# First block's attention for all 512 tokens ahead of the feed-forward, with the second q piece loaded before v

## The chip, the cores and the metric

The kernel runs on one core of a Trainium2 chip. The metric is device time in microseconds (us), the median of several runs of the same kernel. A profiled execution gives the trace from which all rows below are taken.

## The reference

Two stages: attention with keys and values projected along the sequence (1024 positions to 64), then a two-layer feed-forward net with a sigmoid-weighted gelu. There are 8 batches, 8 heads, 1024 positions, head size 64; the feed-forward goes from 512 to 2048 and back.

```python
k_proj = np.einsum('ks,bhsd->bhkd', E, k)
v_proj = np.einsum('ks,bhsd->bhkd', F, v)
scores = scale * np.matmul(q, k_proj.transpose(0, 1, 3, 2))
attn = np.exp(scores - max); attn = attn / (sum(attn) + 1e-09)
x = np.matmul(attn, v_proj)          # heads side by side: 8192 tokens x 512
h = x @ w_in                         # 512 -> 2048
out = (h * (1.0 / (1.0 + np.exp(-1.702 * h)))) @ w_out   # 2048 -> 512
```

## The kernel before

The 8192 tokens are worked in 16 blocks of 512 (index `j` or `h`), two blocks to a batch. A block's attention gives `xT`, 512 features by 512 tokens, in four chunks, one for each pair of heads (`p`). `ffn1` (L377) makes one of 16 feature chunks (`fc`) of the hidden layer with four matmuls over `w_in` and a gelu on ACT. `ffn2` (L395) sums over the 16 chunks with `w_out` for one of four token groups (`n`), and ACT copies the result out.

The schedule is written by hand. The code emits instructions in program order, and each engine works through its own queue in that order. `fill` and `at(j, slot, ...)` (L424 to L507) put attention work of later blocks between the feed-forward steps of block `j`: a slot is the index of an `ffn1` step, or `O`/`Q` plus the index of an `ffn2` part. Tiles in PSUM come from two pools of four buffers each, `ps_f` (`f_tile`) and `ps_x`; a tile that takes a used buffer waits until its reader is done.

Loads are issued by POOL through one queue, in the order of L91 to L106: k in three pieces, the first quarter of q's positions (two of eight), v in three pieces, the second quarter of q, six of eight pieces of `w_in`, the rest of q, the last two pieces of `w_in`, four pieces of `w_out`, then the loads of batch 1. A load is issued when the one eight places earlier has landed.

Block 0 has a start of its own (L431 to L471). `k_piece` projects and transposes k, `q_tr0(g, u, cp)` (L235) transposes a quarter of q on PE, `scores(0, u, half)` (L275) makes scores and exps for 256 tokens, and `v_piece` (L206) projects v for some heads and writes it, masked, into `vx` tiles that have a column of ones behind each head's 64 values. `tok(h, p, half)` (L349) multiplies the exps with `vx` for one pair of heads and two groups of 128 tokens. That gives values and sums together; DVE takes the reciprocal (L359) and multiplies (L361). `x_tr` (L364) transposes the result into `xT` (L369, L371). `warm(n)` (L141) issues matmuls over zeros.

Before the feed-forward starts, only the first 256 tokens (half 0) go through this. Block 0's `ffn1` then runs on half blocks (256 columns): twelve chunks of half 0, twelve of half 1, and so on (L458). The attention of half 1 is placed between the first ones (L459 to L462). The first two chunks of half 0 use a tanh form of the gelu (L390 to L393), while the exp table is still loaded on ACT. The gelu table is loaded after the exps of half 1 (`gelu_table`, L292).

Block 0's `ffn2` begins with two token groups in turn over chunks 0 to 7, 8 to 11 and 12 to 15 (L521).

Batch 1's k is transposed by a DMA on SP's queue (`kv_out`, L229), behind the transposes of its q (`q_dma`, L259). The first reader is `scores(2, ...)`, at the end of block 1's `ffn1`.

Of the kernel before, what the change touches and what calls it, by code (L numbers as in the profile page):

```python
# [9 lines left out]
F32 = mybir.dt.float32  # L10
BF16 = mybir.dt.bfloat16
AF = mybir.ActivationFunctionType
ALU = mybir.AluOpType
# [4 lines left out]
def kernel(ctx, tc, q, k, v, E, F,  # L18
                                                     moe_w_in, moe_w_out, out):
    nc = tc.nc  # L20
    B, H, S, D = q.shape
    KP, _ = E.shape
    DM, DFF = moe_w_in.shape
    P = 128
    J = S // P
    NB2 = S // 512
    HP = H // 2
    KC = DM // P
    FC = DFF // P
    TB = 512  # L30
    JB = TB // P
    NBLK = B * S // TB
    scale = 1.0 / float(D) ** 0.5
# [16 lines left out]
    kt, vt, qt = {}, {}, {}  # L50

    def load_kv(src, dst, b, name, hs=H, js=0, jn=J):
        if b not in dst:
            dst[b] = ldpool.tile([P, H, J, D], BF16, name=name)
        sv = src[b].rearrange("h (p j) d -> p h j d", p=P)
        for h, n in [(h, hs) for h in range(0, H, hs)] if isinstance(hs, int) else hs:
            nc.gpsimd.dma_start(out=dst[b][:, h:h + n, js:js + jn], in_=sv[:, h:h + n, js:js + jn])  # L57
# [35 lines left out]
    make_identity(nc, ident)  # L93
    qt[0] = q_buf(0)
    load_kv(q, qt, 0, "", H, 0, 2)
    load_kv(v, vt, 0, "v_sb", ((0, 4), (4, 2), (6, 2)))
    load_kv(q, qt, 0, "", H, 2, 2)
    for i in range(6):
        load_w_in(i)
    load_kv(q, qt, 0, "", H, JB, JB)  # L100
# [37 lines left out]
    def f_tile(shape, dt=F32):  # L138
        return ps_f.tile(shape, dt, name="f_ps")

    def warm(n):  # L141
        w_ps = ps_x.tile([P, TB], F32, name="x_ps")
        for _ in range(n):
            nc.tensor.matmul(w_ps, zeros[:, :P], zeros, start=True, stop=True)  # L144

# [55 lines left out]
    def vx_of(b, p):  # L201
        if b == 1:
            return vx1[:, 2 * p:2 * p + 2]
        return vx0[0][:, 2 * p:2 * p + 2] if p < 2 else vx0[p - 1]

    def v_piece(h0, n):  # L206

        v_ps = proj0(1, h0, n)
        if n == 4:
            nc.vector.tensor_tensor(vx0[0][:, :, :D], v_ps, mask, op=ALU.mult)  # L210
        else:
            for t in range(n):
                nc.scalar.activation(vx_of(0, h0 // 2)[:, t, :D], v_ps[:, t, :], AF.Identity,
                                     scale=rows[:, h0 % 4 + t:h0 % 4 + t + 1])
# [60 lines left out]
    def scores(h, u, half=None, x=False):  # L275
        b, c = divmod(h, NB2)
        j0, n = (c * JB, JB) if half is None else (c * JB + half * JB // 2, JB // 2)
        ts = slice(j0 * P - c * TB, (j0 + n) * P - c * TB)

        def go():  # L280
            if h not in expT:
                expT[h] = att.tile([P, HP, TB], BF16, name="expT", bufs=3)
            s_ps = [(x_tile() if x else f_tile([P, TB]))[:, :n * P] for _ in range(2)]
            eight(s_ps, [kts[b % 2][:, 2 * u + i, :] for i in range(2)],
                 [q0s[half][u][:, :, i, :] if h == 0 else qT[b][:, j0:j0 + n, 2 * u + i, :]
                   for i in range(2)])
# [59 lines left out]

    xs = {}

    def tok(h, p, half):  # L349
        def go():  # L350
            d_ps = f_tile([P, 4, D + 1]) if (h, half) == (0, 0) and p > 1 else                 ps_x.tile([P, 4, D + 1], F32, name="x_ps")
# [9 lines left out]
            nc.vector.tensor_tensor(xs[h, p, half], d_ps[:, :, :D], rd.to_broadcast([P, 4, D]), op=ALU.mult)  # L361
        return go

    def x_tr(h, p, half):  # L364
        def go():
            x_sb = xs.pop((h, p, half)).rearrange("s (i t) d -> s i (t d)", i=2)
            n_ps = ps_x.tile([P, 2, P], BF16, name="x_ps")
            for i in range(2):
                nc.tensor.transpose(n_ps[:, i, :], x_sb[:, i, :], ident)  # L369
            cp = nc.scalar.copy if (h, half) == (0, 0) else nc.vector.tensor_copy  # L370
            cp(x_of(h)[:, p, half * TB // 2:(half + 1) * TB // 2], n_ps.rearrange("r i s -> r (i s)"))  # L371
        return go


# [2 lines left out]
    def ffn1(j, fc, ts=slice(0, TB)):  # L377
        if j not in gts:
            gts[j] = work.tile([P, FC, TB], BF16, name="gT")
        n = ts.stop - ts.start  # L380
        h_ps = f_tile([P, n])
        for kc in range(KC):
            nc.tensor.matmul(h_ps, w_in_sb[:, kc, fc * P:(fc + 1) * P], xT[j][:, kc, ts],  # L383
                             start=(kc == 0), stop=(kc == KC - 1))
        if j > 0 or ts.start > 0 or fc > 1:
            nc.scalar.activation(gts[j][:, fc, ts], h_ps, AF.Gelu_apprx_sigmoid)  # L386
        else:

            t_sb = work.tile([P, n], F32, name="t_sb", bufs=3)
            nc.scalar.activation(t_sb, h_ps, AF.Tanh, scale=0.851)  # L390
            g = gts[j][:, fc, ts]
            nc.vector.scalar_tensor_tensor(g, t_sb, 1.0, h_ps, op0=ALU.add, op1=ALU.mult)
            nc.vector.tensor_scalar_mul(g, g, 0.5)  # L393

    def ffn2(j, n, fcs):  # L395
        b, c = divmod(j, NB2)
# [29 lines left out]
    def at(j, slot, *fs):  # L426
        fill.setdefault((j, slot), []).extend(fs)

    O = FC
    Q = 2 * FC  # L430
    for h0, n in ((0, 4), (4, 2), (6, 2)):  # L431
        k_piece(h0, n)
    DV, AC = nc.vector.tensor_copy, nc.scalar.copy
# [1 line left out]
    q_tr0(0, 1, AC)  # L435
    warm(2)
    for u in range(2):
        scores(0, u, 0)()
    warm(4)
    v_piece(0, 4)  # L440
    warm(3)
    for p in range(2):
        tok(0, p, 0)()
    v_piece(4, 2)
    warm(1)
    x_tr(0, 0, 0)()
    warm(1)
    tok(0, 2, 0)()
    x_tr(0, 1, 0)()
    v_piece(6, 2)  # L450
    warm(1)
    x_tr(0, 2, 0)()
    tok(0, 3, 0)()
    x_tr(0, 3, 0)()
    q_tr0(1, 0, DV)
    q_tr0(1, 1, DV)

    order = [(half, fc) for fcs in (range(12), range(12, FC)) for half in range(2) for fc in fcs]  # L458
    at(0, 1, scores(0, 0, 1), scores(0, 1, 1, True), gelu_table)  # L459
    for p in range(HP):  # L460
        at(0, 2 + p, tok(0, p, 1))
        at(0, 5 + p, x_tr(0, p, 1))  # L462
    at(0, 20, q_tr(2))
    at(0, 23, q_tr(3))
    for u in range(2):
        at(0, Q, scores(1, u, None, u > 0))
    at(0, Q + 1, gelu_table)
    for p in range(HP):
        at(0, Q + (2, 4, 6, 7)[p], tok(1, p, 0), tok(1, p, 1))
        at(0, Q + (4, 6, 7, 8)[p], x_tr(1, p, 0), x_tr(1, p, 1))  # L470
    at(1, 9, proj(1), kv_out(1))  # L471
    at(1, 1, q_dma(1, 0, JB), q_dma(1, JB, JB))
    for u in range(2):
# [82 lines left out]
```

The softmax here doesn't subtract the row's maximum and nothing guards it: scores larger than these inputs give would overflow.

## Time and profile before

| What | us |
|---|---|
| Median of 7 runs (510.4 to 511.76) | 510.93 |
| The profiled execution's own time | 511.09 |
| Its span, first to last instruction | 509.3 |
| PE busy | 502.6 |
| L415 (`ffn2` matmuls), PE busy, 1008 of them | 226.7 |
| L383 (`ffn1` matmuls), PE busy, 1088 of them | 225.7 |
| ACT busy | 263.7 |
| DVE busy | 158.3 |
| Mean granted TensorE clock | 1.00 |

In the rows that follow, a timeline line has the start in us, the duration in us, the engine, the source line, the operation, the tile written and the tiles read, the shape and a count. A bracket at its end tells how long the engine was idle before it and what ended that. A chain line has start, duration and what ran. "PEld" is PE's weight load, which runs beside matmuls. A matmul's duration in the timeline includes its way through the array; the distance between starts is what a stream of them costs.

### The profile page before, as it was taken

The numbers are of one execution on the slowest core, as the hardware profiler recorded it, in microseconds if no ns is written. First come the engines' busy times: TensorE is split into PE (matmuls) and PEld (weight loads), VectorE is DVE, ScalarE is ACT, GpSimd is POOL, SyncE is SP. The second block draws the span as 40 slices with busy tenths as digits, with TensorE's granted clock in tenths as the row PEclk, the third lists the DMA queues.
The fourth block names the chain that finished last, engine by engine and source line by source line (L and its number), as shares of the span: only waits on it lengthen the run. The fifth ranks groups of instructions, "written<-read, shape, count | busy, mean of one in ns | idle before, by whom it ended". The sixth has DMA issues, their size and how long they took to land.

```text
span 509.3 us, 7242 instructions
## 1 busy us (share of the span) xinstructions
PE 502.6 (99%) x3094; PEld 232.2 (46%) x3094; DVE 158.3 (31%) x219; ACT 263.7 (52%) x443; POOL 78.0 (15%) x97
## 2 busy tenths in 40 slices
PE   8999999999999999999999999999999999999997
PEld 4585445444444444444444444444444444444444
DVE  4523114607161623216161331616214161611000
ACT  1675562664637365471746637374563737244351
POOL 7442051510600510041000510000000000000000
PEclk9999999999999999999999999999999999999999
DMA  9999999999999997598938969090603205060202
GB/s 166 197 203 207 213 157 186 223 200 130 141 239 256 113 195 143 136 154 91 228 62 211 115 111 230 9 244 1 171 1 73 95 5 162 1 167 1 82 1 82
DMA packets 125737, 68.77 MB, mean 135 GB/s; under 512 B 92629, under 2 KB 116565, under 8 KB 123785
## 3 DMA queue, kind: packets, MB, share of 16 engines
q0 software_dynamic: 84400, 29.37, 50.8%
q1 hardware_dynamic: 41224, 38.69, 30.2%
q8 instruction: 24, 0.39, 0.3%
q10 hardware_dynamic: 80, 0.26, 0.2%
q14 instruction: 9, 0.07, 0.0%
HBM read 72.88 MB, written 16.99 MB: 176 GB/s over the span
## 4 chain that ended last, share of the span: by engine, by line
PE 92%; DMA 6%; POOL 1%; issue 0%; DVE 0%; ACT 0%; POOLq 0%
PE f_ps L415 43%; PE f_ps L383 42%; PE f_ps L174 3%; DMA w_in_sb<-in_moe_w_in_dram 2%; DMA v_sb<-in_v_dram 2%; PE f_ps L269 2%; PE x_ps L269 1%; DMA kt<-k_b 1%; PE f_ps L407 1%; PE x_ps L307 1%; POOL k_sb L57 0%; PE x_ps L354 0%; PE x_ps L369 0%; PE f_ps L251 0%; POOL q_even L57 0%
## 5 line engine op out<-in xcount | busy, mean ns | idle before, releaser
L415 PE MATMUL f_ps<-w_out_sb,gT 128*128 128x512 bf16 x1008 | 226.7, 379 | 0.0
L383 PE MATMUL f_ps<-xT,w_in_sb 128*128 128x512 bf16 (+1 forms) x1088 | 225.7, 367 | 0.6 <-ACT gT L386 0.3
L386 ACT ACTIVATE gT<-f_ps 128x512 bf16<-128x512 f32 (+1 forms) x270 | 151.7, 574 | 58.8 <-PE f_ps L383 57.5
L383 PEld LDWEIGHTS <-w_in_sb 128*128 128x128 bf16 x1088 | 105.7, 98 | 116.1 <-DMA w_in_sb<-in_moe_w_in_dram 0.9
L415 PEld LDWEIGHTS <-gT 128*128 128x128 bf16 x1008 | 95.7, 98 | 121.7 <-issue 11.8
L418 ACT COPY o_sb<-f_ps 128x512 f32<-128x512 f32 x63 | 36.9, 586 | 130.7 <-PE f_ps L415 121.0
L342 DVE TENSOR_TENSOR xT<-x_ps,rbc 128x512 bf16<-128x512 f32 x52 | 33.3, 685 | 217.6 <-PE x_ps L269 120.7
L310 DVE RECIPROCAL rden<-x_ps 128x512 f32<-128x512 f32 x26 | 85.3, 3322 | 10.4 <-PE x_ps L307 10.3
L70 POOL DMA_DIRECT2D q_sb<-in_q_dram x48 | 42.0, 905 | 154.9 <-DMA qT<-q_sb 131.3
L288 ACT ACTIVATE expT<-f_ps 128x512 bf16<-128x512 f32 (+1 forms) x58 | 30.1, 573 | 30.4 <-PE f_ps L269 30.3
L288 ACT ACT_TABLE_LOAD x13 | 16.7, 1283 | 4.7 <-PE f_ps L269 4.5
L292 ACT ACT_TABLE_LOAD x14 | 18.0, 1283 | 0.3
L57 POOL DMA_DIRECT2D k_sb<-in_k_dram x10 | 8.5, 857 | 54.8 <-PE f_ps L174 53.1
L228 DVE CAST k_b<-f_ps 64x512 bf16<-64x512 f32 x7 | 4.8, 683 | 37.8 <-PE f_ps L174 37.8
L174 PE MATMUL f_ps<-k_sb,eft 128*64 128x512 bf16 x56 | 13.4, 382 | 0.0
L174 PE MATMUL f_ps<-v_sb,eft 128*64 128x512 bf16 x56 | 13.4, 382 | 0.0
L144 PE MATMUL x_ps<-zeros 128*128 128x512 bf16 x34 | 11.4, 459 | 1.2 <-DVE zeros L115 1.2
L409 DVE COPY o_sb<-f_ps 128x256 f32<-128x256 f32 (+1 forms) x2 | 0.7, 358 | 37.3 <-issue 36.9
L269 PE MATMUL f_ps<-qT,kt 64*32 64x512 bf16 x208 | 10.6, 386 | 0.4 <-DMA kt<-k_b 0.4
L269 PE MATMUL x_ps<-expT,vq 64*32 64x512 bf16 x208 | 10.2, 378 | 0.0
L361 DVE TENSOR_TENSOR x_sb<-x_ps,rd 128x256 bf16<-128x256 f32 x22 | 9.3, 425 | 0.8
L359 DVE RECIPROCAL rd<-x_ps 128x4 f32<-128x4 f32 x22 | 3.8, 175 | 17.8 <-PE x_ps L354 17.8
(71 smaller groups left out, 128.3 us busy)
## 6 DMA issues: line engine op xcount, KB each, us to landing
out_dram<-o_sb SPq DMA_DIRECT2D x15, 1024.0 KB
rbc<-rdr SPq DMA_DIRECT2D x26, 512.0 KB
k_sb<-in_k_dram POOLq DMA_DIRECT2D x7, 1024.0 KB, 14.0
v_sb<-in_v_dram POOLq DMA_DIRECT2D x7, 1024.0 KB, 18.2
q_sb<-in_q_dram POOLq DMA_DIRECT2D x48, 128.0 KB, 5.5
w_in_sb<-in_moe_w_in_dram POOLq DMA_DIRECT2D x8, 256.0 KB, 12.2
w_out_sb<-in_moe_w_out_dram POOLq DMA_DIRECT2D x4, 512.0 KB, 14.7
q_even<-in_q_dram POOLq DMA_DIRECT2D x8, 128.0 KB, 10.2
```

The costliest lines, as they stand in the source:

```text
L70: nc.gpsimd.dma_start(out=qt[b][:, j], in_=qv[:, j])
L144: nc.tensor.matmul(w_ps, zeros[:, :P], zeros, start=True, stop=True)
L174: nc.tensor.matmul(kvps[b][r], eft(j, slice(e * KP, (e + 1) * KP)), (kt, vt)[e][b][:, :, j, :], start=(j == 0), stop=(j == J - 1))
L269: nc.tensor.matmul(outs[i][r.start + c:r.start + c + 32], lhsTs[i][ri, c:c + 32], rhss[i][ri], start=True, stop=True)
L288: nc.scalar.activation(expT[h][:, 2 * u + i, ts], s_ps[i], AF.Exp, scale=scale)
L292: nc.scalar.preload_act_table(AF.Gelu_apprx_sigmoid)
L310: nc.vector.reciprocal(rden[:, e, :], d_ps[e])
L342: nc.vector.tensor_tensor(x_of(h)[:, 2 * u + i, :], n_ps[i], rbc[h][:, 2 * u + i, :], op=ALU.mult)
L383: nc.tensor.matmul(h_ps, w_in_sb[:, kc, fc * P:(fc + 1) * P], xT[j][:, kc, ts], start=(kc == 0), stop=(kc == KC - 1))
L386: nc.scalar.activation(gts[j][:, fc, ts], h_ps, AF.Gelu_apprx_sigmoid)
L415: nc.tensor.matmul(o_ps[n], gts[j][:, fc, n * P:(n + 1) * P], w_out_sb[:, fc, :], start=(fc == 0), stop=(fc == FC - 1))
L418: nc.scalar.copy(osb[j][:, n, :], o_ps.pop(n))
```

## The change

- The second quarter of q is loaded ahead of v.
- Scores and exps of half 1 move ahead of v's projection, and so does the load of the gelu table.
- The sums of the exps are computed by matmuls of their own with the ones columns (two columns wide), for two token groups and all pairs at a time (`sums0`); DVE takes 16 reciprocals per partition at once.
- The values come from `tok0`, one pair of heads and all four token groups at a time, with two multiplications on DVE. `x_tr0` transposes four groups, copied by ACT in one piece for pairs 0 to 2, by DVE in two pieces for pair 3.
- Block 0's `ffn1` has two half-width chunks for each half, then 14 whole ones. The tanh form is gone.
- Block 0's `ffn2` begins with three token groups in turn, by quarters of the chunks. The slots of block 1's attention and of the later q transposes are moved to fit.

```diff
     load_kv(q, qt, 0, "", H, 0, 2)
+    load_kv(q, qt, 0, "", H, 2, 2)
     load_kv(v, vt, 0, "v_sb", ((0, 4), (4, 2), (6, 2)))
-    load_kv(q, qt, 0, "", H, 2, 2)
...
-    def warm(n):
-        w_ps = ps_x.tile([P, TB], F32, name="x_ps")
+    def warm(n, f=False):
+        w_ps = f_tile([P, TB]) if f else ps_x.tile([P, TB], F32, name="x_ps")
...
+    rd0 = consts.tile([P, 2, HP, 2, 2], F32, name="rd0")
+
+    def sums0(half):
+        d_ps = ps_x.tile([P, HP, 2, 2], F32, name="x_ps")
+        for p in range(HP):
+            for i in range(2):
+                t = 2 * half + i
+                nc.tensor.matmul(d_ps[:, p, i, :], expT[0][:, p, t * P:(t + 1) * P],
+                                 vx_of(0, p)[:, :, D:].rearrange("r t o -> r (t o)"), start=True, stop=True)
+        nc.vector.reciprocal(rd0[:, half], d_ps)
+
+    def tok0(p):
+        n_ps = ps_x.tile([P, 2, 2, 2, D], F32, name="x_ps")
+        for t in range(JB):
+            nc.tensor.matmul(n_ps[:, t // 2, t % 2].rearrange("s t d -> s (t d)"),
+                             expT[0][:, p, t * P:(t + 1) * P], vx_of(0, p)[:, :, :D], start=True, stop=True)
+        xs[p] = work.tile([P, 2, 2, 2, D], BF16, name="x0_sb", bufs=4)
+        for a in range(2):
+            nc.vector.tensor_tensor(xs[p][:, a], n_ps[:, a], rd0[:, a, p, :, :, None].to_broadcast([P, 2, 2, D]),
+                                    op=ALU.mult)
+
+    def x_tr0(p, parts, cp):
+        n_ps = ps_x.tile([P, JB, P], BF16, name="x_ps")
+        for g in range(parts):
+            for t in range(g * JB // parts, (g + 1) * JB // parts):
+                nc.tensor.transpose(n_ps[:, t, :], xs[p][:, t // 2, t % 2].rearrange("s t d -> s (t d)"), ident)
+            sl = slice(g * JB // parts, (g + 1) * JB // parts)
+            cp(x_of(0)[:, p, sl.start * P:sl.stop * P], n_ps[:, sl].rearrange("r t s -> r (t s)"))
...
-        if j > 0 or ts.start > 0 or fc > 1:
-            nc.scalar.activation(gts[j][:, fc, ts], h_ps, AF.Gelu_apprx_sigmoid)
-        else:
...
+        nc.scalar.activation(gts[j][:, fc, ts], h_ps, AF.Gelu_apprx_sigmoid)
...
-    Q = 2 * FC
+    order = [(half, fc) for half in range(2) for fc in range(2)] + [(None, fc) for fc in range(2, FC)]
+    Q = len(order)
...
     for u in range(2):
-        scores(0, u, 0)()
-    warm(4)
-    v_piece(0, 4)
-    warm(3)
-    for p in range(2):
-        tok(0, p, 0)()
-    v_piece(4, 2)
-    warm(1)
-    x_tr(0, 0, 0)()
-    warm(1)
-    tok(0, 2, 0)()
-    x_tr(0, 1, 0)()
-    v_piece(6, 2)
-    warm(1)
-    x_tr(0, 2, 0)()
-    tok(0, 3, 0)()
-    x_tr(0, 3, 0)()
+        scores(0, u, 0, u > 0)()
     q_tr0(1, 0, DV)
     q_tr0(1, 1, DV)
-    order = [(half, fc) for fcs in (range(12), range(12, FC)) for half in range(2) for fc in fcs]
-    at(0, 1, scores(0, 0, 1), scores(0, 1, 1, True), gelu_table)
+    warm(1)
+    sums0(0)
+    for u in range(2):
+        scores(0, u, 1, u > 0)()
+    gelu_table()
+    v_piece(0, 4)
+    sums0(1)
+    warm(1, True)
+    tok0(0)
+    tok0(1)
+    v_piece(4, 2)
+    warm(2, True)
+    x_tr0(0, 1, AC)
+    tok0(2)
+    v_piece(6, 2)
+    warm(1, True)
+    x_tr0(1, 1, AC)
+    tok0(3)
+    warm(1, True)
+    x_tr0(2, 1, AC)
+    warm(1, True)
+    x_tr0(3, 2, DV)
+    warm(2, True)
+    at(0, 13, q_tr(2))
+    at(0, 15, q_tr(3))
+    for u in range(2):
+        at(0, Q + 1, scores(1, u, None, True))
+    at(0, Q + 3, gelu_table)
     for p in range(HP):
-        at(0, 2 + p, tok(0, p, 1))
-        at(0, 5 + p, x_tr(0, p, 1))
-    at(0, 20, q_tr(2))
-    at(0, 23, q_tr(3))
...
-        at(0, Q + (2, 4, 6, 7)[p], tok(1, p, 0), tok(1, p, 1))
-        at(0, Q + (4, 6, 7, 8)[p], x_tr(1, p, 0), x_tr(1, p, 1))
+        at(0, Q + (4, 6, 9, 11)[p], tok(1, p, 0), tok(1, p, 1))
+        at(0, Q + (6, 9, 11, 12)[p], x_tr(1, p, 0), x_tr(1, p, 1))
...
-            parts[:4] = [(n, fcs) for fcs in (range(8), range(8, 12), range(12, FC)) for n in range(2)]
+            parts[:6] = [(n, range(4 * g, 4 * g + 4)) for g in range(4) for n in range(3)]
```

More of the change, by code (lines that the diff above doesn't have):

```diff
@@ L347 @@
     xs = {}
+    rd0 = consts.tile([P, 2, HP, 2, 2], F32, name="rd0")
[23 more added lines that the diff above has]
+            cp(x_of(0)[:, p, sl.start * P:sl.stop * P], n_ps[:, sl].rearrange("r t s -> r (t s)"))
     def tok(h, p, half):
         def go():
-            d_ps = f_tile([P, 4, D + 1]) if (h, half) == (0, 0) and p > 1 else                 ps_x.tile([P, 4, D + 1], F32, name="x_ps")
+            d_ps = ps_x.tile([P, 4, D + 1], F32, name="x_ps")
             for i in range(2):
@@ L369, in go @@
                 nc.tensor.transpose(n_ps[:, i, :], x_sb[:, i, :], ident)
-            cp = nc.scalar.copy if (h, half) == (0, 0) else nc.vector.tensor_copy
-            cp(x_of(h)[:, p, half * TB // 2:(half + 1) * TB // 2], n_ps.rearrange("r i s -> r (i s)"))
+            nc.vector.tensor_copy(x_of(h)[:, p, half * TB // 2:(half + 1) * TB // 2], n_ps.rearrange("r i s -> r (i s)"))
         return go
@@ L384, in ffn1 @@
                              start=(kc == 0), stop=(kc == KC - 1))
-        if j > 0 or ts.start > 0 or fc > 1:
-            nc.scalar.activation(gts[j][:, fc, ts], h_ps, AF.Gelu_apprx_sigmoid)
-        else:
[L389 to L393, printed above, removed]
+        nc.scalar.activation(gts[j][:, fc, ts], h_ps, AF.Gelu_apprx_sigmoid)
     def ffn2(j, n, fcs):
@@ L437 @@
     for u in range(2):
-        scores(0, u, 0)()
-    warm(4)
-    v_piece(0, 4)
-    warm(3)
-    for p in range(2):
-        tok(0, p, 0)()
-    v_piece(4, 2)
-    warm(1)
-    x_tr(0, 0, 0)()
-    warm(1)
-    tok(0, 2, 0)()
-    x_tr(0, 1, 0)()
-    v_piece(6, 2)
-    warm(1)
-    x_tr(0, 2, 0)()
-    tok(0, 3, 0)()
-    x_tr(0, 3, 0)()
+        scores(0, u, 0, u > 0)()
     q_tr0(1, 0, DV)
     q_tr0(1, 1, DV)
-    order = [(half, fc) for fcs in (range(12), range(12, FC)) for half in range(2) for fc in fcs]
-    at(0, 1, scores(0, 0, 1), scores(0, 1, 1, True), gelu_table)
-    for p in range(HP):
-        at(0, 2 + p, tok(0, p, 1))
-        at(0, 5 + p, x_tr(0, p, 1))
-    at(0, 20, q_tr(2))
-    at(0, 23, q_tr(3))
[L465 to L468, printed above, removed]
-        at(0, Q + (2, 4, 6, 7)[p], tok(1, p, 0), tok(1, p, 1))
-        at(0, Q + (4, 6, 7, 8)[p], x_tr(1, p, 0), x_tr(1, p, 1))
+    warm(1)
[26 more added lines that the diff above has]
+    at(0, Q + 3, gelu_table)
+    for p in range(HP):
+        at(0, Q + (4, 6, 9, 11)[p], tok(1, p, 0), tok(1, p, 1))
+        at(0, Q + (6, 9, 11, 12)[p], x_tr(1, p, 0), x_tr(1, p, 1))
     at(1, 9, proj(1), kv_out(1))
```

## The prediction

> **What bounds the kernel now.** I read the page's busy shares first, then the chain of waits in order of time, then the timeline of the first 30 us on PE and POOL, and last the busy time by stage.
>
> ```profile
> span 509.3 us, 7242 instructions
> PE 502.6 (99%) x3094; PEld 232.2 (46%) x3094; DVE 158.3 (31%) x219; ACT 263.7 (52%) x443; POOL 78.0 (15%) x97
> PE 92%; DMA 6%; POOL 1%; issue 0%; DVE 0%; ACT 0%; POOLq 0%
> ```
>
> PE is the bound nearly everywhere, so a change at the start is worth what it moves the moment from which PE runs without a gap, plus the PE work that it takes out after that moment. The chain in order of time shows where PE is not the bound:
>
> ```profile
> 5.73 10.46 DMA v_sb<-in_v_dram
> 16.47 11.50 DMA w_in_sb<-in_moe_w_in_dram
> 28.02 4.98 PE f_ps L383 x44
> ...
> 55.42 8.63 PE f_ps L383 x40
> ...
> 66.68 6.60 DMA kt<-k_b
> ```
>
> Up to 28.02 us transfers decide: first v, then w_in. From 28.02 on it is PE, with one later transfer on the chain, kt at 66.68 us. On PE, the last steps before the first feed-forward matmul (L383) are these:
>
> ```profile
> 14.89 1.05 PE L182 MATMUL f_ps<-v_sb,ffs 128*128 128x256 bf16 x8
> ...
> 20.36 0.29 PE L369 MATMUL x_ps<-ident,x_sb 128*128 128x128 bf16 x2 [0.74 <-DVE x_sb L361]
> ...
> 21.28 1.05 PE L383 MATMUL f_ps<-xT,w_in_sb 128*128 128x256 bf16 x8
> ```
>
> The first v projection starts at 14.89, ended by the wait for v; the feed-forward starts at 21.28. POOL issues a load only when an earlier one has landed, so its releasers tell when each landed:
>
> ```profile
> 12.61 0.74 POOL L86 DMA_DIRECT2D w_in_sb<-in_moe_w_in_dram  x1 [0.69 <-DMA q_even<-in_q_dram]
> 15.12 0.74 POOL L86 DMA_DIRECT2D w_in_sb<-in_moe_w_in_dram  x1 [1.78 <-DMA v_sb<-in_v_dram]
> 16.47 0.74 POOL L86 DMA_DIRECT2D w_in_sb<-in_moe_w_in_dram  x1 [0.60 <-DMA v_sb<-in_v_dram]
> 17.77 0.89 POOL L57 DMA_DIRECT2D q_even<-in_q_dram  x1 [0.56 <-DMA v_sb<-in_v_dram]
> 20.19 0.75 POOL L86 DMA_DIRECT2D w_in_sb<-in_moe_w_in_dram  x1 [1.54 <-DMA q_even<-in_q_dram]
> ```
>
> The reader is to see the steps: v's three pieces let go at 15.12, 16.47 and 17.77, the second q piece only at 20.19. The busy time by stage (elapsed us, then busy us of PE, PEld, DVE, ACT, POOL):
>
> ```profile
> 21.28:38.98 17.70, 17.12 (x193) 14.35 (x193) 6.33 (x20) 13.69 (x36) 8.43 (x11) 1.00 1.37 201
> 38.98:55.25 16.27, 16.27 (x114) 8.13 (x112) 6.16 (x24) 6.91 (x11) 4.03 (x5) 1.00 1.48 196
> ```
>
> Block 0's first feed-forward layer takes 17.70 us, its second 16.27, the latter without a gap.
>
> **What the Trainium skill says.** "ScalarE: Activation LUTs", section "Table sets", says that cheap functions such as identity and copy are in every table set, and "What ACT_TABLE_LOAD costs" gives 1283 ns and a drain of about 1380 ns. The trace has 1283 ns at L292 (23.87) and the next gelu at 25.17, so no drain shows; I take 1.28 us, and no reload for the copies that follow the moved load. "DMA: Bandwidth & Descriptors", section "Queues, rings and completion order", says that each engine takes turns among its rings. This bears on the instruction queue: the trace shows one q8 packet of 0.02 MB between 17.3 and 17.5 us, and the q piece then in flight took 2.42 us from step to step (17.77 to 20.19), where the first q piece of the same size took 1.43 (11.18 to 12.61). I charge about 1 us of that to this packet. "TensorE: Matmul & The Clock Gate", section "The HAM clock gate", says that about 3.4 us of idle halve PE's clock. The trace's PE waits 0.74 us before 20.36 and the granted clock stays 1.00.
>
> **The change part by part.** *Saved after the start.* Of the 17.70 us, the half-width matmuls are 128, at 0.111 each (44 in 28.02 to 32.92). The two q transposes cost 2 x 0.57. The rest, 2.3 us, is block 0's second token half (scores, four toks, four transposes, about 1.5 us) and waits (about 0.8: the gelu table, w_in). After: 16 half-width matmuls (1.78), 56 whole ones at 0.2157 (8.63/40, so 12.08), the same q transposes (1.14): 15.0 us. Saved: 2.70 us. A w_in piece is now used in 1.73 us against one arriving every 1.35, so no w_in wait follows if the start is after 21.3. w_out's first quarter releases POOL at 36.66; it is needed 15.0 us after the start, at 38 or later. The tanh form of gelu for two tiles goes, six small instructions with two gelus in their place; ACT and DVE hid them beside PE, so it counts nothing. The second layer in three token groups by quarters has the same 64 matmuls: 16.27 stays. Its scores use four x_ps buffers; ACT frees them (1.28 + 4 x 0.57, about 3.6 us after the first layer) before the first tok, four parts plus scores or 4.9 us in. Were that cover gone, it would cost up to 1 us; I take nothing.
>
> *Moved ahead of v.* The second q piece is loaded before v. POOL's issue takes 0.9 us and stays well ahead of the transfers. Its transfer pushes v by 1.43 us if it costs as the first q piece; two runs of small packets in a row may cost up to 1.75. The order of w_in is untouched, since q goes ahead of it in both. The q8 packet comes at PE's 240th instruction or so (243 had begun at 17.4). That count is reached in the changed kernel near 15.5 us, while v is in flight instead of q. I take it to hit v's first piece as it hit q, another 0.97 us. The bounds are 0 and 1.1. So v's first projection starts at V = 14.88 + 1.43 + 0.97 = 17.3 (bounds 16.3 and 17.7). PE is ready for it at about 16: q lands at 13.9, transposes 0.57, copies by 15.5, sums 0.45, scores 0.5.
>
> *From V to the feed-forward.* Spacings are those of the timeline: projection of four heads 0.89, of two heads 0.44; PE to DVE or ACT 0.2; masking multiply 0.43; four small matmuls 0.22; rows activation pair 0.52; multiply 0.42, every 0.35 when in a row; copy of 256 columns 0.28, of 512 0.58; warm-up matmul 0.22. V + 1.51: v masked on DVE, while PE does sums (0.45, set by eight weight loads at 0.055; bounds 0.4 and 0.8, covered until 1.51) and a warm-up. V + 1.56 to 2.00: tok0 of pairs 0 and 1. To 2.44: two heads projected; ACT ready at 3.16; beneath it two warm-ups and the first transposes. 3.22 to 3.44: tok0 of pair 2. To 3.88: last projection; ACT, after a 512-wide copy that ends at 3.89, at 4.60. 4.66: tok0 of pair 3; DVE's first half at 5.51, second at 5.86. Transposes of the first half at 5.57, copied by 6.18. In the instruction order of the changed kernel, the second half's transposes wait for that copy: 6.23 to 6.34. Two warm-ups: 6.77. The feed-forward starts at V + 6.77 = 24.07. The moved table load lies before V on ACT (exps end near 17, load to 18.4, ACT next needed at V + 2.6 = 19.9): hidden.
>
> *Sum.* Start 24.07 - 21.28 = 2.79 us later; 2.70 saved; +0.09. The profiled execution is 511.09 (span 509.3 and 1.8 around it), so 511.2 on its own scale; it lies 0.16 above the median of 510.93, so 511.0.
>
> *Later.* kt's transfer ended PE's wait of 0.41 us at 73.32. The kt issue follows PE; the q transposes queued before it on SP (57.50, 7.05 us) wait for q, which doesn't move. An earlier PE would therefore wait longer there, by at most what it gained; a later one doesn't.
>
> **The rivals.** *The instruction packet misses v's critical piece or falls on an engine with slack.* V is 16.3 to 16.6, start 23.1 to 23.4, and the change gains 0.6 to 0.9: 510.2. For it: nothing before 17.4 shows on which engine it falls. Against: it cost q about 1 us. *kt eats it:* with that gain, PE waits at 73 us instead: 510.9. Against: kt's issue at 66.68 is 2.1 us after SP is free. *Slower: PE's clock.* Between 14 and 17.3 us PE has transposes, two-column sums, narrow scores and gaps of about 1.5 us, with one warm-up in place of seven. If this passes for idle, PE runs at half speed for a window of 3.4 us, an estimate from the clock page named above: it loses 1.7 us in dense work. This gives 512.7. It decides from the point where the granted clock drops at all. Against: from 18 to 21.3 us before, PE has much the same mix and keeps 1.00.
>
> **How the numbers follow.** Forecast case (within about 0.5 of 511.0) 0.48; packet misses, 0.27; kt eats it, 0.10; clock or an equally long chain, 0.15. A measurement tells 0.2% (1.0 us) from nothing. The forecast's tails give 0.02 faster and 0.03 slower; the missed packet passes 1.0 us with a chain 0.3 shorter than summed, 0.12 of its 0.27; the clock case is slower in 0.13. So faster 0.14, same 0.70, slower 0.16. The range reaches to the missed packet with a shorter chain (509.9) and partly to the clock case (512.2).
>
> **What would show it.** v's first projection at 17.3 (16.4 in the rival), the first L383 near 24.1, ffn2 (now L436) 15.0 us later, no w_in wait, a PE wait before the last transposes, and kt's wait near 0.4 us. Wrong would be a granted clock under 1.00 before 25 us, sums over 0.8 us, or gaps inside the second layer.

## The result, and the profile after

| What | before | after |
|---|---|---|
| Median, us | 510.9 (34 runs, 510.24 to 512.0) | 515.54 (14 runs, 511.57 to 517.41) |
| Ratio to before, 95% interval | | 1.0075 [1.006, 1.009] |
| Profiled execution: own time, span, us | 511.09, 509.3 | 512.09, 510.2 |
| Mean granted clock of the profiled execution | 1.00 | 1.00 |

The change makes the kernel 0.75% slower. The profiled execution shows only a part of this. It is among the shortest of the changed kernel, and its clock is 1.00. Executions of the changed kernel differ in the mean granted clock. In the series of the table 11 of 14 had 0.993 to 0.997 (513.37 us and more), and three had 1.00 (511.57 to 512.07). In a second series of 19 (e1 below), 12 had 0.999 or 1.000 and a median of 512.08 us, and 7 had 0.993 to 0.997 and a median of 516.31. Both groups belong to the result, so two things are to be explained: about 1 us at full clock, and some 4 us more where the clock falls.

The page of the changed kernel, its span and the busy shares:

```profile
span 510.2 us, 7135 instructions
PE 501.7 (98%) x3053; PEld 227.3 (45%) x3053; DVE 155.2 (30%) x207; ACT 262.2 (51%) x428; POOL 78.0 (15%) x97
```

PE has 0.9 us less work than before and a span 0.9 us longer: 1.8 us more of waiting. The timeline of PE in the start:

```profile
17.38 1.05 PE L182 MATMUL f_ps<-v_sb,ffs 128*128 128x256 bf16 x8 [0.75 <-DMA v_sb<-in_v_dram]
...
23.64 0.27 PE L375 MATMUL x_ps<-ident,x_sb 128*128 128x128 bf16 x2 [0.38 <-DVE xT L377]
23.75 0.59 PE L144 MATMUL f_ps<-zeros 128*128 128x512 bf16 x2
24.18 2.13 PE L412 MATMUL f_ps<-xT,w_in_sb 128*128 128x256 bf16 x17
```

v is projected at 17.38 and the feed-forward starts at 24.18, against 14.89 and 21.28 before. The busy time of block 0's two layers, in the columns used before:

```profile
24.18:39.36 15.18, 15.18 (x106) 7.82 (x105) 1.44 (x3) 9.29 (x17) 7.34 (x9) 1.00 1.35 202
39.36:55.63 16.27, 16.27 (x113) 8.12 (x112) 6.16 (x24) 6.99 (x10) 3.62 (x5) 1.00 1.50 195
```

The first layer takes 15.18 us instead of 17.70, with no gap, and the second 16.27 as before. Block 1 starts at 55.63, 0.38 later than before. The next loss is in the chain in order of time:

```profile
64.43 1.89 PE f_ps L174 x16
...
67.05 7.15 DMA kt<-k_b
...
74.25 0.41 PE f_ps L269 x8
...
74.87 3.56 PE f_ps L436 x16
```

The timeline has PE's wait for it in the bracket:

```profile
74.25 0.41 PE L269 MATMUL f_ps<-qT,kt 64*32 64x512 bf16 x8 [0.96 <-DMA kt<-k_b]
```

kt (batch 1's k, transposed by DMA) was issued 0.37 us later than before and took 7.15 us instead of 6.60. PE waited 0.96 us for it instead of 0.41. The delay at block 1, 0.38, and the longer wait, 0.55, make the 0.9 us of the span.

### The profile page after: what moved, and what is told of

It reads as the page before. It is cut to its first block, busy times and chain, and to the rows that moved or that the text cites. A ratio compares the mean times of both kernels' runs of the same rounds, so it can differ in the third digit from the quotient of the medians.

```text
span 510.2 us, 7135 instructions
## 1 busy us (share of the span) xinstructions
PE 501.7 (98%) x3053; PEld 227.3 (45%) x3053; DVE 155.2 (30%) x207; ACT 262.2 (51%) x428; POOL 78.0 (15%) x97
## 4 chain that ended last, share of the span: by engine, by line
PE 94%; DMA 4%; POOL 1%; DVE 0%; issue 0%; ACT 0%; POOLq 0%
PE f_ps L436 43%; PE f_ps L412 42%; PE f_ps L174 3%; DMA v_sb<-in_v_dram 2%; PE f_ps L269 2%; PE x_ps L269 1%; DMA kt<-k_b 1%; PE f_ps L428 1%; PE x_ps L307 1%; POOL k_sb L57 0%; PE f_ps L182 0%; PE x_ps L384 0%; PE x_ps L399 0%; POOL q_even L57 0%; PE x_ps L364 0%; PE f_ps L144 0%
## 5 line engine op out<-in xcount | busy, mean ns | idle before, releaser
L412 PEld LDWEIGHTS <-w_in_sb 128*128 128x128 bf16 x1032 | 100.6, 98 | 120.0 <-issue 0.6
L288 ACT ACTIVATE expT<-f_ps 128x512 bf16<-128x512 f32 (+1 forms) x54 | 28.4, 579 | 31.1 <-PE f_ps L269 31.0
L174 PE MATMUL f_ps<-k_sb,eft 128*64 128x512 bf16 x56 | 13.4, 382 | 0.0
L174 PE MATMUL f_ps<-v_sb,eft 128*64 128x512 bf16 x56 | 13.4, 382 | 0.0
L144 PE MATMUL x_ps<-zeros 128*128 128x512 bf16 x25 | 8.6, 476 | 1.2 <-DVE zeros L115 1.2
L57 POOL DMA_DIRECT2D v_sb<-in_v_dram x10 | 8.4, 846 | 5.0 <-DMA q_sb<-in_q_dram 2.9
L174 PEld LDWEIGHTS <-eft 128*64 128x64 bf16 x112 | 5.7, 109 | 7.3 <-issue 3.0
## 6 DMA issues: line engine op xcount, KB each, us to landing
rbc<-rdr SPq DMA_DIRECT2D x26, 512.0 KB
v_sb<-in_v_dram POOLq DMA_DIRECT2D x7, 1024.0 KB, 17.3
w_out_sb<-in_moe_w_out_dram POOLq DMA_DIRECT2D x4, 512.0 KB, 14.7
```

Source lines behind the costliest of these rows:

```text
L174: nc.tensor.matmul(kvps[b][r], eft(j, slice(e * KP, (e + 1) * KP)), (kt, vt)[e][b][:, :, j, :], start=(j == 0), stop=(j == J - 1))
```

## The experiments

Three theories stood at first, and the expectations name them by letters. Theory A (later S) put the low clock into the start, where PE has gaps and narrow matmuls; D, in e6, is a variant of it. Theory B took it for a by-product of transfers that land at varying times. Theory C (later K) put the loss at the wait for kt. For the first six runs it was not yet known where the clock falls.

**e1: the changed kernel again.** No edit.

> The changed kernel again, for its spread and a second trace. Theory A (PE's clock is halved for a stretch in the start in most executions): spans from 509.8 to 515.6 us, and every span over 511.5 us goes with a mean granted clock under 0.999; where the trace is of such a run, the clock by stretches of 2 us is under 1.00 somewhere between 14 and 25 us and 1.00 after it, and PE's 256-column matmuls there start 0.22 us apart in place of 0.11. Theory B (transfers land at varying times, the clock is a by-product): times vary while the clock is 1.000, and the wait for v or k varies by up to 4 us. Theory C (the clock falls later, at the wait for kt near 74 us): the drop is seen between 70 and 80 us.

Measured: 512.43 (511.2 to 516.73, 19 runs), ratio 1.0044 [1.0025, 1.0063]. The low clocks are there again, in 7 of 19. The kernel before beside it had one in 4 of 66. In this series every execution of 513.48 us or more has a clock of 0.997 or less, and every shorter one 0.999 or more. The changed kernel's own median therefore depends on how many of its executions fall. The trace is of one at full clock (wait for kt 0.81 us), so it does not show where.

**e2: PE kept busy while v is awaited.**

```diff
     gelu_table()
+    warm(5, True)
     v_piece(0, 4)
```

> The changed kernel with five more 512-column matmuls over zeros (1.1 us) in the wait for v. Theory A: the clock stays 1.000 in every execution, all times within 1 us of each other, near 511.5 us (the unthrottled time of the changed kernel, 512.09 in its profiled run, 511.6 at best), at most 0.4 later where the filler outlasts the wait. Theory B: spread from 511.6 to 517 as without it. Theory C: the same spread, since the stretch near 74 us is unchanged.

Measured: 512.04 (511.43 to 516.57, 20 runs), 1.0036 [1.0017, 1.0055]; 6 of 20 at 0.993 to 0.997. Covering the largest gap of the start left the low clocks where they were. Its trace, at full clock, also shows a start in which k lands on time. POOL's releasers and PE:

```profile
8.49 0.75 POOL L86 DMA_DIRECT2D w_in_sb<-in_moe_w_in_dram  x1 [0.45 <-DMA k_sb<-in_k_dram]
...
16.56 1.04 PE L182 MATMUL f_ps<-v_sb,ffs 128*128 128x256 bf16 x8
```

In the profiled execution of the changed kernel k's first piece let go of POOL at 9.60. Here it is 8.49, as before the change (8.57), and v is projected at 16.56 instead of 17.38.

**e3: the kernel before without its seven zero matmuls ahead of and behind v's first projection.**

```diff
-    warm(4)
     v_piece(0, 4)
-    warm(3)
```

> The kernel before without the seven zero matmuls around its first v projection. They fill waits, so without a change of the clock the time stays at 510.9. Theory A: the clock falls below 0.999 in part of the executions and these are 2 to 5 us longer. Theories B and C: 510.9 and clock 1.000.

Measured: 511.49 (510.78 to 513.9, 15 runs), 1.001 [0.9999, 1.0021]; one run of 15 at 0.997. With the zero matmuls it was 4 of 66. Emptying PE at the same place of the kernel before does not bring the clock down either.

**e4: the kernel before with the second q piece loaded ahead of v.**

```diff
     load_kv(q, qt, 0, "", H, 0, 2)
-    load_kv(v, vt, 0, "v_sb", ((0, 4), (4, 2), (6, 2)))
     load_kv(q, qt, 0, "", H, 2, 2)
+    load_kv(v, vt, 0, "v_sb", ((0, 4), (4, 2), (6, 2)))
```

> The kernel before with the second q piece loaded ahead of v, nothing else. The first v projection moves from 14.89 to about 16.3 us and the feed-forward's start from 21.28 to about 22.7, so 512.3 at clock 1.000. Theory A: the longer wait before v (1.5 us more) may lower the clock in part of the executions, these then 2 us or more longer. Theory B: 512.3 with a spread of several us at clock 1.000. Theory C: 512.3 and no spread.

Measured: 512.49 (511.56 to 515.04, 19 runs), 1.0032 [1.0022, 1.0041]. v is projected 1.72 us later (16.61) and the feed-forward starts 1.67 later (22.95); the median is 1.7 above that of the kernel before beside it (510.79). A later start is paid in full, and one run of 19 has a low clock.

**e5: the changed kernel without the nine zero matmuls that stand between its second q transposes and the feed-forward.**

```diff
-    warm(1)
     sums0(0)
...
-    warm(1, True)
     tok0(0)
...
-    warm(2, True)
     x_tr0(0, 1, AC)
...
-    warm(2, True)
     at(0, 13, q_tr(2))
```

(The three `warm(1, True)` ahead of `x_tr0(1, ...)`, `x_tr0(2, ...)` and `x_tr0(3, ...)` go too.)

> The changed kernel without its nine zero matmuls between the second q transposes and the feed-forward. Theory A (a drop of PE's clock in the start, set by how much dense matmul work PE has there): nearly every execution shows a mean clock under 0.999 and takes 514 to 518 us, and the trace shows the stretch with the clock at one half between 14 and 30 us. Theory B (transfers vary, the clock is a by-product): the same share of long executions as the changed kernel, about a third to four fifths, and those at clock 1.000 0.4 us shorter, since two zero matmuls before the feed-forward are gone.

Measured: 516.54 (514.84 to 517.0, 4 runs), 1.009 [1.0058, 1.0122], clocks 0.993, 0.993, 0.993 and 0.996. The feed-forward starts at 22.34, 1.84 us earlier than in the profile of the changed kernel, and the kernel is the slowest so far. The times are what theory A expected, but the place is not. The trace, an execution with the low clock, shows it. Busy time by stretches of 2 us (elapsed, PE busy, granted clock, then two columns on the DMA):

```profile
72.00:74.00 2.00, 0.00 (x0) 1.00 1.62 182
74.00:76.00 2.00, 0.00 (x0) 0.69 1.08 159
76.00:78.00 2.00, 1.41 (x18) 0.50 2.17 162
78.00:80.00 2.00, 2.00 (x6) 0.50 2.43 155
80.00:82.00 2.00, 2.00 (x7) 0.60 2.43 155
82.00:84.00 2.00, 2.00 (x14) 1.00 2.02 171
```

The clock is 1.00 through the start. Worked out from the shares of 0.69 and 0.60, it is halved at 74.8 us, in block 1, while PE does nothing, and comes back at 81.6. The chain in order of time says what PE waited for, and what the `ffn2` matmuls behind the wait took:

```profile
53.38 10.59 DMA q_sb<-in_q_dram
...
64.05 2.75 SPq L259
...
66.86 9.69 DMA kt<-k_b
...
76.59 0.63 PE f_ps L269 x5
...
77.64 5.53 PE f_ps L436 x16
```

```profile
76.59 0.63 PE L269 MATMUL f_ps<-qT,kt 64*32 64x512 bf16 x8 [5.14 <-DMA kt<-k_b]
```

Block 1 starts 1.5 us earlier than before the change, but kt lands at 76.55 instead of 73.28. PE waits 5.14 us, and the 16 `ffn2` matmuls take 5.53 us instead of 3.56 in the changed kernel's profile.

**e6: nine more zero matmuls, in every wait of the start.** Here `warm(1)` becomes `warm(2)`, a `warm(4, True)` stands ahead of `v_piece(0, 4)`, and five more, one or two at a time, are added further on.

> The changed kernel with nine more zero matmuls, put in every wait of PE between the second q transposes and the feed-forward (before v, before the first values, before the last pair's values, between the last two transposes). Theory A: long executions (over 513 us) become rare, under one in ten; the others stay at 511.3 to 512.5, as the changed kernel at full clock. Theory B: long executions as often as with the changed kernel. Theory D (the drop comes from the waits before 14 us, which both kernels have): as often as with the changed kernel too, but the trace of a long execution has the clock at one half before 14 us.

Measured: 515.11 (511.27 to 516.86, 12 runs), 1.0063 [1.0037, 1.0088], 7 of 12 at 0.993 to 0.997. Theory A expected less than one in ten. With the waits of the start filled, the clock falls about as often as without (18 of 33 in the changed kernel's two series). The chain of its trace, again one with a low clock:

```profile
66.68 9.00 DMA kt<-k_b
...
76.36 5.25 PE f_ps L438 x16
```

```profile
75.73 0.41 PE L269 MATMUL f_ps<-qT,kt 64*32 64x512 bf16 x8 [3.27 <-DMA kt<-k_b]
```

PE waited 3.27 us for kt. The 16 `ffn2` matmuls behind it took 5.25 us, where the same 16 take 3.56 in the chains of before and after. That is 1.69 us lost, as much as 3.4 us at half clock cost. With e2, e3, e5 and e6 the start is out as the place of this loss.

Why does an earlier PE get kt later? Rows of the kernel before and of e5 answer it. POOL's loads for batch 2, which PE's projection (L174) sets free, first before, then in e5:

```profile
66.19 0.87 POOL L57 DMA_DIRECT2D k_sb<-in_k_dram  x1 [11.48 <-PE f_ps L174]
```

```profile
64.73 0.88 POOL L57 DMA_DIRECT2D k_sb<-in_k_dram  x1 [10.48 <-PE f_ps L174]
```

Before, kt is issued 0.49 us behind this load (66.68). In e5 the load comes 1.5 us earlier, but kt at 66.86: SP is still busy with q's transposes, since q's last piece landed at 63.97 (10.59 us after its issue; this load took 6.6 before). So kt stands 2.1 us behind a stream of loads. What slowed q's piece is, by all signs, the 1 MB store of block 0's output, which an earlier PE lets go earlier. Load and store before the change, and the store in e5:

```profile
53.84 0.87 POOL L70 DMA_DIRECT2D q_sb<-in_q_dram  x1 [4.15 <-DMA v_sb<-in_v_dram]
...
56.06 0.36 SPq L422 DMA_DIRECT2D out_dram<-o_sb  x1
```

```profile
54.61 0.36 SPq L443 DMA_DIRECT2D out_dram<-o_sb  x1
```

The traces of all the kernels in this text divide without exception. In eleven of them the store comes 2.15 us or more behind q's last piece, and this piece lands in 6.5 to 6.6 us. In seven (e5, e6, e7, e9, e10, e12 and e16) the store comes 1.80 us or less behind it, and the piece takes 9.4 to 10.6 us. The store was not moved by itself. So it is not PE's earliness alone that counts: in e2 and e6 block 1 starts at the same time (54.80), but q was issued at 53.07 in e2 and at 53.92 in e6, and PE waits 1.50 us for kt in e2 and 3.27 in e6.

**e7 and e8: kt ahead of the second half of q's transposes on SP,** in the changed kernel and in the kernel before.

```diff
-    at(1, 9, proj(1), kv_out(1))
-    at(1, 1, q_dma(1, 0, JB), q_dma(1, JB, JB))
+    at(1, 9, proj(1), kv_out(1), q_dma(1, JB, JB))
+    at(1, 1, q_dma(1, 0, JB))
```

> The changed kernel with the second half of batch 1's q transposes put behind the kt transpose on SP's queue (it is first read 13 us later). Theory K (the loss arises in block 1: SP is held by the q transposes, whose last piece of q lands at a fixed time, so kt's issue does not follow an earlier PE): SP issues kt at about 66 us as soon as k_b is there, PE's wait for kt falls under 0.5 us, no execution has a clock under 0.999, and times lie at 509.8 to 511.3 us. Theory S (the loss arises in the start, before 25 us): a third or more of the executions stay at 513 to 517 us.

> The same edit on the kernel before. Theory K: its wait for kt of 0.4 us shrinks or stays; 510.3 to 510.9 us, and its few executions at 513.4 us (clock 0.997) vanish. Theory S: the few at 513.4 stay.

Measured: e7 512.33 (512.18 to 513.2, 5 runs), 1.0035 [1.0021, 1.0048]; e8 513.09 (512.59 to 513.24, 5 runs), 1.0043 [1.0031, 1.0056]. All ten at clock 1.0. The waits of PE in e7 (total, times, longest):

```profile
PE f_ps L174 <- DMA v_sb<-in_v_dram: 1.4, 1, 1.4
PE f_ps L269 <- DMA kt<-k_b: 0.6, 1, 0.6
```

kt is issued at 65.86, as soon as it is ready, and still takes 6.79 us, since the loads of batch 2 begin at 65.38. A new wait comes up at 91 us, for v of batch 2, whose load goes out 0.9 us later (78.85 instead of 77.92). No clock fell in these ten runs, but nothing is won: 509.8 to 511.3 and 510.3 to 510.9 were expected.

**e9: PE made later.** Eight zero matmuls (1.73 us) at the beginning of block 1: `at(1, 0, lambda: warm(8, True))`.

> The changed kernel with eight zero matmuls (1.73 us of PE) added in block 1, between its first two feed-forward chunks. Theory K: block 1 runs later, so the k load of batch 2 comes later and kt's issue is no longer behind it by as much; PE's wait for kt falls to 0.5 us or less, the executions at 514 to 517 us become rare, and the median falls below that of the changed kernel measured with it (512.4 to 515.5) to about 512, in spite of the added work. Theory S: 1.7 us longer than the changed kernel, with the same share of long executions.

Measured: 512.9 (512.21 to 513.32, 5 runs), 1.004 [1.0027, 1.0052], all at clock 1.0; the wait for kt is 1.2 us, more than the 0.5 expected. With 1.73 us of useless work added the kernel is at 512.9, against 515.54 and 512.43 in the two series without it, and none of the five has a low clock. This agrees with e5 and e6, that the early executions lose, but five runs don't prove it.

**e10: the loads of batch 2 held on POOL until kt has landed.**

```diff
-    at(1, 9, proj(1), kv_out(1))
+    def hold():
+        nc.gpsimd.tensor_copy(hold_sb, kts[1][:, 0, :4])
+
+    hold_sb = consts.tile([P, 4], BF16, name="hold_sb")
+    at(1, 9, proj(1), kv_out(1), hold, lambda: load(2))
```

> The changed kernel with the loads of batch 2 held on POOL until kt has landed. Theory K with the k load of batch 2 as the cause of kt's late landing: kt lands 4 to 5 us after its issue in place of 7 to 9.7, PE's wait is 0.5 us or less, no long executions, 510.0 to 511.5 us. If the q transposes alone are to blame, kt's issue stays late (66.9) and PE still waits 1 to 2 us, long executions remain. Theory S: as the changed kernel.

Measured: 513.35 (512.28 to 516.53, 5 runs), 1.0059 [1.0034, 1.0083], two of five at 0.993 and 0.996. On POOL and PE:

```profile
68.48 0.19 POOL L496 COPY hold_sb<-kt 128x4 bf16<-128x4 bf16 x1 [14.13 <-DMA kt<-k_b]
```

```profile
91.50 0.38 PE L174 MATMUL f_ps<-v_sb,eft 128*64 128x512 bf16 x1 [2.09 <-DMA v_sb<-in_v_dram]
```

kt, issued at 66.09, has landed by 68.48. Alone it takes at most 2.4 us, and beside the loads of batch 2 it takes 6.5 to 9.7. This shows the collision. The time isn't gained, because the held loads then make PE wait 2.09 us for v. Two of the five still had a low clock, though kt's wait was gone. The wait for v may be the reason, but the trace is of an execution at full clock and doesn't show it.

**e11, e12, e13: batch 1's k transposed on PE.** This removes the transfer from the path without moving any other. The edit is the same in the changed kernel (e11), in e5 (e12) and in the kernel before (e13):

```diff
-    def k_tr(k_b, p0):
+    kbs = {}
+
+    def k_tr(k_b, p0, i=0):
...
-        nc.vector.tensor_copy(kts[0][:, p0:p0 + n, :], t_ps)
+        nc.vector.tensor_copy(kts[i][:, p0:p0 + n, :], t_ps)
...
-            nc.sync.dma_start_transpose(out=kts[b % 2], in_=k_b.rearrange("k h d -> k (h d)"))
+            if b == 1:
+                kbs[b] = k_b
+            else:
+                nc.sync.dma_start_transpose(out=kts[b % 2], in_=k_b.rearrange("k h d -> k (h d)"))
...
     at(1, 9, proj(1), kv_out(1))
+    at(1, 11, lambda: k_tr(kbs.pop(1), 0, 1))
```

> The changed kernel, with batch 1's k transposed on TensorE (four transposes of 64 x 128 at the twelfth step of block 1's first layer and one VectorE copy into kt) in place of the DMA transpose. Nothing in block 1 waits for a DMA transpose of k any more. If the wait for kt is the cause: no wait at L269 near 74 us, the granted clock 1.0 in every run, no run above 513.5, and the median is the profiled 512.09 less the 0.96 of the wait plus the transposes' four times 0.06 to 0.2: 511.4 to 512.0, with some runs (those that start early) at 510.5. If the granted clock falls for another reason, which sits in the start: a third of the runs stay at clocks of 0.993 to 0.997 and between 513.4 and 517.

> The version without the nine zero matmuls of the start (which took 516.54 with a wait of 5.1 us for kt), with the same k of batch 1 on TensorE. If the wait for kt and the clock that falls in it are all of its loss: the clock stays 1.0, block 1 starts near 53.8 as it did there, and the time is 512.09 less 1.84 of the earlier start less 0.96 plus 0.5: 509.8, which is below both kernels. If the missing zero matmuls cost clock elsewhere, or if the time gained is lost at the next transfer (v of batch 2, whose load is held by the loads before it), it stays at 511 to 514.

> The same edit on the kernel before, whose wait for kt is 0.41: 510.9 less 0.41 plus 0.2 to 0.8, so 510.7 to 511.3, and no run at a clock of 0.997, where 4 of 66 had one. It says what the edit itself costs. If the edit brings a cost of its own (the accumulators' buffers, VectorE), it is over 511.5 here as well.

| Kernel | median, us (range of 22 runs) | ratio, 95% interval | runs under 0.999 |
|---|---|---|---|
| e11, change with k on PE | 510.62 (510.11 to 511.3) | 0.9978 [0.9968, 0.9988] | 0 of 22 |
| e12, e5 with k on PE | 511.15 (509.73 to 512.24) | 0.9989 [0.9977, 1.0001] | 4 of 22 |
| e13, before with k on PE | 510.75 (510.24 to 513.31) | 0.9991 [0.9978, 1.0003] | 1 of 22 |
| before, beside them | 511.52 (510.13 to 514.4, 59 runs) | | 4 of 59 |

PE and DVE in e11:

```profile
67.83 0.29 PE L199 MATMUL f_ps<-ident,k_b 64*128 64x64 bf16 x4
...
73.33 0.41 PE L274 MATMUL f_ps<-qT,kt 64*32 64x512 bf16 x8
```

```profile
68.43 0.29 DVE L201 COPY kt<-f_ps 128x256 bf16<-128x256 bf16 x1
```

kt is ready at 68.72, 4.6 us before it is wanted, for four transposes that take 0.22 us of PE. No wait, no low clock, and the loss is gone. e12, the version that lost most, comes down by 5.4 us (across two series). The kernel before in this series is 0.6 us above its median elsewhere, so e11 is better set against e13, of the same series: 510.62 and 510.75. Without the wait for kt, the change itself is worth 0.13 us, which these runs can't tell from nothing. e12 is not settled: its full-clock runs fall into two groups (nine from 509.73 to 510.60, nine from 511.14 to 511.67), and four have 0.996 or 0.997. The one trace of it (span 508.2, clock 1.00) shows the cause of neither.

**e14, e15, e16: the wait without a transfer.** e11 took the wait and the transfer away together. Here k stays on PE, and DVE, idle at that place, works ahead of its copy into kt.

```diff
-    at(1, 11, lambda: k_tr(kbs.pop(1), 0, 1))
+    hold = consts.tile([P, TB], F32, name="hold")
+
+    def hold_kt():
+        nc.vector.memset(hold, 1.0)
+        for _ in range(2):
+            nc.vector.reciprocal(hold, hold)
+        k_tr(kbs.pop(1), 0, 1)
+    at(1, 11, hold_kt)
```

(e15 adds two multiplications behind the reciprocals; e16 has three reciprocals.)

> The version with batch 1's k transposed on TensorE (510.62, no wait), in which VectorE, idle at that place, works ahead of its copy into kt: a memset and two reciprocals of 128 x 512 (3.32 each). The copy ends near 75.6 in place of 68.7, and TensorE, which wants kt at 73.3, waits some 2.2 us; no transfer is part of this wait. If a wait has to fill a window[...] to bring the clock down: the clock stays 1.0 in every run and the time is 510.62 + 2.2 = 512.8. If any wait there does it: clocks of 0.997 and 514 to 515.

> The same with two multiplications of 128 x 512 more (0.69 each at most): the copy ends near 76.9 and the wait is some 3.5 us. If the length of the wait alone decides: a mixture, runs at 1.0 with 514.1 and runs at 0.997 with one window at half clock, 1.7 more, 515.8; whether a run falls depends on where the window's edge lies. If transfers are needed for the clock to fall: 514.1 in every run, at 1.0.

> The same with three reciprocals: the copy ends near 79.0 and the wait is some 5.5 us, as long as the 5.1 of the version without the zero matmuls. If the length of the wait alone decides: the clock is 0.997 or lower in nearly every run, one or two windows at half clock just after the wait, and the time is 510.62 + 5.5 + 1.7 to 3.4: 517.8 to 519.5. If transfers are needed: 516.1 at 1.0.

| Kernel | wait in the trace, us | median, us (4 runs each) | clocks |
|---|---|---|---|
| e11 | none | 510.62 | 0.999 to 1.000 |
| e14 | 2.80 | 514.72 (512.72 to 515.76) | 0.999, 0.997, 0.996, 0.996 |
| e15 | 4.25 | 516.87 (516.54 to 517.48) | 0.996, 0.996, 0.993, 0.993 |
| e16 | 6.19 | 518.57 (517.88 to 518.9) | 0.993, 0.993, 0.993, 0.992 |

In e14, PE and the stretches after it:

```profile
76.23 0.41 PE L274 MATMUL f_ps<-qT,kt 64*32 64x512 bf16 x8 [2.80 <-DVE kt L201]
```

```profile
74.00:76.00 2.00, 0.00 (x0) 1.00 1.60 171
76.00:78.00 2.00, 1.77 (x19) 0.68 2.27 152
78.00:80.00 2.00, 2.00 (x6) 0.50 2.42 154
80.00:82.00 2.00, 2.00 (x11) 0.97 2.34 161
```

The wait ends at 76.23 and the half clock runs from about 76.7 to 80.1, so PE pays for it in the work that follows. In e16 it lies partly within the wait itself:

```profile
74.00:76.00 2.00, 0.00 (x0) 0.71 1.80 177
76.00:78.00 2.00, 0.00 (x0) 0.50 2.41 155
78.00:80.00 2.00, 1.33 (x17) 0.50 2.43 155
80.00:82.00 2.00, 2.00 (x7) 0.58 2.22 166
```

A wait is enough for it, no transfer is needed. I had held a wait well under 3.4 us to be safe, and three of e14's four runs fell. The wait itself was longer than reckoned, 2.80 instead of 2.2: the two reciprocals took 6.74 us instead of 6.65, and the memset 0.48. Against e11's 510.62, from another series, the waits of 2.80, 4.25 and 6.19 cost 4.1, 6.25 and 7.95 us of median: the wait, and 1.3 to 2.0 us on top.

## Why the prediction was wrong

The forecast was 511.0, at most 512.2; the result is 515.54. The sum for the start and for block 0 came out within 0.3 us: block 1 starts 0.38 later in the profile, where 0.09 was reckoned. In the start this was luck. The step that failed is the paragraph "Later": an earlier PE "would therefore wait longer there, by at most what it gained; a later one doesn't". With it failed the assumption that a low clock could only come from the start. None of the signs that the prediction named as wrong showed up; its "kt's wait near 0.4 us" is the one that missed, with 0.96.

- *First v projection at 17.3.* The profiled execution has 17.38, but by another cause. The second q piece costs 1.44 us (POOL's steps 13.61 to 15.05), as reckoned. The 0.97 charged to the instruction packet (2.42 less 1.43 is 0.99) did not fall on v's first piece: this piece let POOL go 2.57 us after q, against 2.51 before. The packet was misread: in the kernel before it stands at 17.1 to 17.2 us, not 17.3 to 17.5. In the changed kernel it comes at 18.4 to 18.5, with some 300 of PE's instructions begun, not with the 240th near 15.5; by then v's first piece has landed. What made up the rest is k, 1.0 us late in this execution; why, is open. Where k is on time, as in e2 and e11, v is projected at 16.56 and 16.31, as in the rival "misses v's critical piece" (16.3 to 16.6). But in e11 the packet, at 17.1 to 17.2, stands where v's second piece is under way, and that piece is late:

```profile
16.31 1.05 PE L182 MATMUL f_ps<-v_sb,ffs 128*128 128x256 bf16 x8 [0.79 <-DMA v_sb<-in_v_dram]
...
19.19 0.61 PE L182 MATMUL f_ps<-v_sb,ffs 128*128 128x128 bf16 x8 [0.70 <-DMA v_sb<-in_v_dram]
```

The feed-forward of e11 therefore starts at 23.97, near the forecast's 24.07 all the same; in e2 it starts at 23.34.

- *From V to the feed-forward, 6.77.* Measured 24.18 less 17.38: 6.80, with the predicted wait before the last transposes (0.38).
- *First layer 15.0, second 16.27.* Measured 15.18 and 16.27, with no wait for w_in. These terms held, and the +0.09 in all agrees with e11 against e13 (-0.13), where the wait for kt is out of the way, within what these runs can tell.
- *kt.* Two assumptions were wrong. "q, which doesn't move" moves: in e5 its last piece landed at 63.97. And kt's landing does not follow PE: PE's own projection releases the loads of batch 2, behind which kt queues, and the end of PE's block 0 releases the store that meets q's last piece. A later PE waited 0.55 more in the profiled execution (0.38 later), and 0.07 more in e4 (1.33 later). An earlier one (e5, 1.5 us) waited 4.7 us more, three times what it gained. The bound "PE waits at most what it gained" treats the landing as a fixed time, and it isn't.
- *The clock.* The rival named the mechanism and its size: half speed for a window of 3.4 us, 1.7 us lost (e6: 1.69). But it looked in the start, at 14 to 17.3 us, where no trace shows a clock under 1.00. It should have been joined to "kt eats it", the one transfer that the chain still had after the start. The Trainium skill, "TensorE: Matmul & The Clock Gate", section "The HAM clock gate", says that the window runs freely, not from the kernel's start. That agrees with the mixed executions: one and the same kernel has the clock fall in some and not in others (e14: 512.72 at 0.999, and 515.76 at 0.996).

The changed kernel's excess is then: at full clock 512.08 (e1) against 510.62 without the wait (e11), 1.5 us; and 4.2 us more (516.31 less 512.08) where the clock falls. The first figure is rough, because the kernel before differs by 0.7 us between these two series (510.79 and 511.52). What remains argued is that the low-clock executions of the changed kernel itself have the long wait: its own traces are all at full clock (waits of 0.81 and 0.96 us), and the waits of 3.27 and 5.14 are those of its variants e6 and e5. For it speaks e10, which is the changed kernel up to the loads of batch 2. Its block 1 starts at 54.47 us, its q piece takes 9.4 us, and SP is free of q's transposes only at 66.04, against 64.55 before.

## What to carry to other kernels

When a change moves a busy engine in time, look for the next transfer whose neighbours are released by that same engine; its landing is not fixed, and an earlier engine can meet it later than before. Look also for stores that the engine lets go earlier: here a load issued shortly ahead of one took 9.4 to 10.6 us instead of 6.5. Price a wait of a few microseconds on PE with the clock behind it: here one of 2.8 us cost about 4. A small transpose on the engine itself (0.22 us here) can be the cheaper way to get an operand than a transfer that must share its queues with the next batch's loads.

## What the runs showed of the hardware that was not expected

- In e14, whose trace has a wait of 2.80 us, the clock fell in three of four runs; by the shares in that trace it was then halved for 3.4 us, longer than the wait. Waits of up to 1.50 us for kt, and one of 2.09 us for v (e10), stood in traces whose clock was 1.00.
- One DMA transpose of k (64 x 512, bf16) landed in at most 2.4 us alone, and in 6.5 to 9.7 us beside the loads of the next batch. SP's own time on it was 1.17 to 1.25 us in these.
- The last 128 KB piece of q landed in 6.5 to 6.6 us in the eleven traces in which a 1 MB store was issued 2.15 us or more behind it, and in 9.4 to 10.6 us in the seven in which the store came 1.80 us or less behind it.
- Taking nine zero matmuls off PE's start (e5) gave 516.54 and a low clock in 4 of 4 runs, where the changed kernel had one in 18 of 33; adding eight in the middle (e9) gave 512.9 and none in 5.
